# An adaLN block with linear attention and a bilinear GLU: modulation columns by halves and the first k product block by block

## The chip, the cores and the metric

The kernel runs on one core of one Trainium2 chip. The metric is the device time of one execution in microseconds; the median of three runs before the change is 566.74 us (566.28 to 568.02). Everything is computed in float32. Large products are made from float32 values that are split into a rounded high half (type fp32r, which TensorE multiplies in one pass) and a low half (value minus high half); a product of two split operands is three matmuls: high x high, high x low, low x high.

## The reference

Sequence S = 2048, width D = 512, 32 heads of 16, hidden width 1376. Cut to what matters for the change:

```python
mod = (_silu(c) @ w_mod).reshape(c.shape[0], 6, 1, -1)
sa, ca, ga, sb, cb, gb = (mod[:, 0], mod[:, 1], mod[:, 2], mod[:, 3], mod[:, 4], mod[:, 5])
h = _layernorm(x, axis=-1) * (1 + ca) + sa
x = x + ga * _A_ref(h, A_wqkv, A_wo)
h = _layernorm(x, axis=-1) * (1 + cb) + sb
x = x + gb * _B_ref(h, B_w_gate, B_w_up, B_w_down)
```

`_A_ref` is linear attention: q, k and v are products of h with the three parts of wqkv; phi(t) = where(t > 0, t + 1, exp(t)) + 1e-6 is applied to q and k; kv = sum over tokens of phi(k) times v, z = sum over tokens of phi(k); the output is (phi(q) kv) / (phi(q) z), times wo. `_B_ref` is ((h w_gate) * (h w_up)) w_down.

## The kernel before

Tokens are handled in 4 chunks of 4 token tiles of 128 tokens; D is cut into KD = 4 blocks of 128. The whole order of work is written out by hand: each engine runs its instructions in the order in which the program issues them, and waits at semaphores. Matmul results lie in two pools of four PSUM banks (`acc_bank()`, `bank()`); all large tiles in SBUF come from one pool of 99.

The opening, the part that the change touches (L342 to L474):

- All loads of the opening are issued by SyncE (SP) in one queue, in this order: chunk 0 of x (4 tiles, with c behind the first), the scale columns' part of w_mod (`raw_ca`, 4 loads of 128 x 512), the shift columns' part (`raw_sa`, 4), the k weights (`raw_k`, 4), chunk 1 of x, the q weights, the v weights, chunks 2 and 3 of x. Each is 256 KB in rows of 2 KB.
- `keep_on(n)` (L139) issues n matmuls of zeros on TensorE whose result nobody reads.
- Layer norm of chunk 0 (`Norm`): `stats` on VectorE, `rstd_of` (a power on GpSimd), `nmr_of` (minus mean times rstd, VectorE), `xhat` (the normalised tile, ScalarE), `transpose_token` (TensorE, token tile j into all four blocks' banks).
- The modulation columns: w_mod has its input rows as partition p and index k, so silu(c) @ w_mod is, per column, a sum over k and over partitions. `mod_acc` (L154) does the sum over k on VectorE, with one scale and three multiply-adds of 512 columns; `mod_col` (L161) does the sum over partitions on TensorE, four one-column matmuls against `ones`; `col_out` (L167) copies it out and adds 1 for the scale. This is done for the scale (ca), then for the shift (sa), before the first block can be modulated.
- `modulated` (L264) applies scale and shift to the transposed block k on ScalarE, and makes high and low halves; `split_raw` makes those of the weights (high on ScalarE, low on VectorE).
- The k product of token tiles 0 and 1 is `product2` (L198), two banks in turn, block by block; tiles 2 and 3 follow with `proj` (L285), one tile at a time (L424, L429).
- Then the loop over the 16 token tiles i (L425): k products two tiles ahead (`ahead`), `k_split_x` and `k_split` (high and low halves of the normalised tile and of phi(k)), `t_tile` (L325: phi(k) transposed times the normalised tile, into four accumulators `tacc`), `k_phi` and `q_a`/`q_b` (phi from a bank: two ScalarE passes and one VectorE pass), `z_add`, the next chunk's norm in pieces, and `extra[i]` (q, v and o weights' halves, the other four modulation vectors). Four q products of chunk 0 stand at i = 3, 4, 6 and 7 (`q_at`, L423).

Behind the loop come the attention output (L545 to L660), the second layer norm and the GLU (L663 to L1062), which the change does not touch.

Of the kernel before, what the change touches and what calls it, by code (L numbers as in the profile page):

```python
# [14 lines left out]
P = 128  # L15
# [7 lines left out]
def tile_adaln_block(  # L23
# [17 lines left out]
    NJ = 4  # L41
# [23 lines left out]
    def f32(ap):  # L65
        return ap.bitcast(F32)
# [33 lines left out]
    nc.gpsimd.memset(eps_z, S * EPS_PHI)  # L100
    half = consts.tile([P, NJ], F32, name="half")
# [21 lines left out]
    raw_ca = load_mod(1)  # L123
    raw_sa = load_mod(0)
    raw_k = load_qkv(1)
# [88 lines left out]
    class Norm:  # L214
# [30 lines left out]
        def xhat(self, *js):  # L245
            for j in js:
                self.n[j] = B("n")
                nc.scalar.activation(self.n[j], self.tiles[j], AF.Identity,  # L248
                                     scale=self.rstd[:, j:j + 1], bias=self.nmr[:, j:j + 1])
# [49 lines left out]

    def k_split_x(i):  # L300
# [44 lines left out]
    acc_ca, acc_sa = B("f"), B("f")  # L345
    keep_on(18)
    n0.stats(0, 1)
    n0.rstd_of(0, 2)
    silu()
    n0.stats(2)  # L350
    n0.nmr_of(0, 2)
    n0.xhat(0, 1)
    n0.stats(3)
    n0.rstd_of(2, 4)
    mod_acc(acc_ca, raw_ca, [0])
    n0.nmr_of(2, 4)
    n0.xhat(2, 3)
    n0.transpose_token(0)
    keep_on(3)
    n0.transpose_token(1)  # L360
    keep_on(3)
    n0.transpose_token(2)
    mod_acc(acc_ca, raw_ca, [1, 2, 3])
    keep_on(1)
    n0.transpose_token(3)
    ps_ca = mod_col(acc_ca, acc_bank())
    mod_acc(acc_sa, raw_sa, [0, 1, 2, 3])
    ca = col_out(1, ps_ca, 1.0)
    keep_on(4)
    ps_sa = mod_col(acc_sa, acc_bank())  # L370
    keep_on(8)
    wk.append(split_raw(raw_k[0]))
    sa = col_out(0, ps_sa, 0.0)
    nx = Norm(xts[1])
    nx.stats(0)
    n0.modulated(ca, sa, 0, cast=nc.vector)
    wk.append(split_raw(raw_k[1]))
    n0.modulated(ca, sa, 1, cast=nc.vector)
    wk.append(split_raw(raw_k[2]))
    n0.modulated(ca, sa, 2)  # L380
    nx.stats(1)
    wk.append(split_raw(raw_k[3]))
    n0.modulated(ca, sa, 3)
    ps0, ps1 = acc_bank(), acc_bank()
    product2((ps0, ps1), [[(cut(n0.t[k], j * P, (j + 1) * P), wk[k]) for k in range(KD)] for j in range(2)])
    nx.stats(2, 3)
    nx.rstd_of()
    k_split_x(0)
    k_phi(0, ps0)
    nx.nmr_of()  # L390
    k_phi(1, ps1)
    k_split(0)
    nx.xhat(0, 1)

    tacc = [acc_bank() for _ in range(KD)]
    rows, cols = {}, {}
# [7 lines left out]
    def mod_part(v, *ks):  # L404
        if 0 in ks:
# [3 lines left out]
    extra = {0: lambda: (wq.extend(split_raw(r) for r in raw_q[0:1]),),  # L409
             1: lambda: (wq.extend(split_raw(r) for r in raw_q[1:2]),),  # L410
             2: lambda: (wq.extend(split_raw(r) for r in raw_q[2:4]),),
             4: lambda: (wv.extend(split_raw(r) for r in raw_v[0:1]),),
# [10 lines left out]
    q_at = {3: 0, 4: 1, 6: 2, 7: 3}  # L423
    ahead = {2: proj(2, wk)}  # L424
    for i in range(NT):  # L425
        ch, j = divmod(i, NJ)
        more = ch + 1 < NCH
        if i == 0:
            ahead[3] = proj(3, wk)  # L429
        elif i > 1:  # L430
# [3 lines left out]
        if more and j == 0:  # L434
            nx.xhat(2)
        if i + 1 < NT:
            k_split_x(i + 1)
        if more and j == 0:
            nx.xhat(3)
# [7 lines left out]
        if ch + 2 < NCH and j == 2:  # L447
            nx2 = Norm(xts[ch + 2])
            nx2.stats(0, 1)
        if ch + 2 < NCH and j == 3:  # L450
            nx = nx2
            nx.stats(2, 3)
            nx.rstd_of()
            nx.nmr_of()
            nx.xhat(0, 1)
        if i + 2 < NT:
            k_phi(i + 2, ahead.pop(i + 2))
        else:
            q_a(i + 6 - NT, ahead.pop(i + 2))
            q_b(i + 6 - NT)  # L460
        if i in q_at:
            q_a(q_at[i], qps)
            q_b(q_at[i])
        if i + 1 < NT:
            z_add(i + 1)
        if i == NT - 1:
# [623 lines left out]
```

## Time and profile before

| | |
|---|---|
| median of three runs | 566.74 us (566.28 to 568.02) |
| the profiled execution's own time | 566.38 us |
| its span in the profile | 564.6 us |
| TensorE busy (matmul) | 556.7 us, 99% of the span |
| TensorE weight loads | 456.0 us, 81% |
| VectorE, ScalarE, GpSimd busy | 67%, 52%, 37% |
| mean granted TensorE clock | 0.995 |

The profile is of one execution. Times are microseconds from the span's start; engines are PE (TensorE matmul), PEld (its weight loads, which run beside the matmuls), DVE (VectorE), ACT (ScalarE), POOL (GpSimd) and SP (SyncE, which issues the DMAs). A line such as `L784 PE MATMUL bank<-h,w` reads: source line 784, engine, operation, written tile <- read tiles, without buffer numbers. In a timeline the columns are start, length, and then the instruction, with the idle time ahead of it and what ended it in brackets; instructions of one line that follow each other are merged (x8). Matmul lengths overlap: what one costs in a stream is the distance from one start to the next. A float32 matmul against `ones` shows as two records. The chain of waits is followed back from the end of the execution, and its rows stand in order of time. In a windows view each row is a stretch of time, with the busy time and instruction count of each engine, the granted clock (1.00 is full), the DMA engines' busy share and what they moved in GB/s.

### The profile page before, as it was taken

How to read it: one execution, taken by the hardware profiler on the slowest of the kernel's cores; microseconds unless marked ns; L12 is line 12 of the kernel's file. 1: busy time of each engine (PE TensorE's matmuls, PEld its weight loads, DVE VectorE, ACT ScalarE, POOL GpSimd, SP SyncE). 2: the span in 40 equal slices, each digit the busy share in tenths (PEclk: the TensorE clock that was granted, in tenths of full speed). 3: DMA queues.
4: the chain of work that ended last, by engine and by line, in shares of the span. 5: the costliest groups of instructions: out<-in, count | busy, mean ns of one | idle time of the engine just before them, and what ended most of it. 6: DMA issues, size and time to landing. Idle time of an engine off the chain costs nothing.

```text
span 564.6 us, 7390 instructions
## 1 busy us (share of the span) xinstructions
PE 556.7 (99%) x2549; PEld 456.0 (81%) x2549; DVE 380.2 (67%) x643; ACT 293.8 (52%) x530; POOL 207.0 (37%) x224
## 2 busy tenths in 40 slices
PE   7999999999999999999999999999999999999997
PEld 6778888887888888888888888877888888888775
DVE  6876868869898998866555767862555554444653
ACT  3685857546367877662554455453443343344420
POOL 2000000002517745345555544486324555554200
PEclk9899999999999999999999999999999999999999
DMA  8900224200421011142445134699343211200004
GB/s 270 384 17 2 74 75 140 85 0 22 128 71 43 1 48 27 38 131 94 149 150 186 39 121 169 212 350 308 113 130 102 58 48 39 80 0 1 0 1 149
DMA packets 49109, 57.24 MB, mean 101 GB/s; under 512 B 6384, under 2 KB 26864, under 8 KB 49072
## 3 DMA queue, kind: packets, MB, share of 16 engines
q1 hardware_dynamic: 49072, 56.77, 31.2%
q8 instruction: 20, 0.33, 0.2%
q14 instruction: 17, 0.14, 0.1%
HBM read 43.12 MB, written 13.63 MB: 101 GB/s over the span
## 4 chain that ended last, share of the span: by engine, by line
PE 92%; DMA 3%; DVE 3%; SPq 0%; issue 0%; ACT 0%; POOL 0%
PE bank L784 36%; PE acc L621 8%; PE acc L862 7%; PE acc L863 7%; PE acc L864 7%; PE bank L194 5%; PE bank L196 5%; PE bank L195 5%; PE acc L332 2%; PE acc L330 2%; PE acc L331 2%; PE bank L255 2%; DMA h<-side_a 1%; PE bank L596 1%; DMA x<-in_A_x_dram 1%; DMA h<-side_s 1%
## 5 line engine op out<-in xcount | busy, mean ns | idle before, releaser
L784 PE MATMUL bank<-h,w 128*128 128x512 f32 (+1 forms) x924 | 216.3, 391 | 0.2 <-DMA h<-side_s 0.2
L784 PEld LDWEIGHTS bank<-h,w 128*128 128x128 f32 (+1 forms) x924 | 170.6, 185 | 39.5 <-DMA h<-side_s 1.0
L790 ACT ACTIVATE bank<-bank 128x512 f32<-128x512 f32 (+1 forms) x44 | 25.6, 581 | 151.9 <-PE bank L784 151.8
L770 POOL TENSOR_TENSOR w<-raw,w 128x256 fp32r<-128x256 f32 (+3 forms) x44 | 46.3, 1051 | 158.4 <-ACT w L763 151.1
L810 DVE TENSOR_TENSOR phi<-bank,g 128x512 f32<-128x512 f32 (+1 forms) x22 | 15.2, 689 | 83.6 <-PE bank L784 79.9
L862 PE MATMUL acc<-w,kh 128*128 128x512 f32 (+1 forms) x176 | 68.6, 390 | 0.0
L863 PE MATMUL acc<-w,kh 128*128 128x512 f32 (+1 forms) x176 | 68.6, 390 | 0.0
L864 PE MATMUL acc<-w,kl 128*128 128x512 f32 (+1 forms) x176 | 68.5, 389 | 0.0
L770 POOL TENSOR_TENSOR w<-t,w 128x512 fp32r<-128x512 f32 (+1 forms) x44 | 57.6, 1308 | 0.0
L869 DVE TENSOR_TENSOR x<-acc,x 128x512 f32<-128x512 f32 x80 | 50.3, 682 | 8.6 <-PE acc L864 8.6
L194 PE MATMUL bank<-w,h 128*128 128x512 f32 x120 | 48.1, 401 | 0.0
L196 PE MATMUL bank<-w,h 128*128 128x512 f32 x120 | 47.0, 392 | 0.0
L195 PE MATMUL bank<-w,h 128*128 128x512 f32 x120 | 46.8, 390 | 0.0
L237 POOL TENSOR_TENSOR rstd<-ve,half 128x4 f32<-128x4 f32 (+3 forms) x12 | 11.1, 925 | 85.9 <-DVE ve L234 68.9
L490 POOL TENSOR_TENSOR f<-h,zb 128x512 f32<-128x512 f32 x12 | 17.1, 1441 | 69.4 <-ACT zb L470 50.8
L621 PE MATMUL acc<-w,xh 128*128 128x512 f32 x128 | 40.7, 399 | 0.0
L862 PEld LDWEIGHTS acc<-w,kh 128*128 128x128 f32 (+1 forms) x176 | 33.0, 188 | 7.0
L864 PEld LDWEIGHTS acc<-w,kl 128*128 128x128 f32 (+1 forms) x176 | 33.0, 188 | 7.0
L863 PEld LDWEIGHTS acc<-w,kh 128*128 128x128 f32 (+1 forms) x176 | 33.1, 188 | 6.9
L752 POOL TENSOR_TENSOR t<-raw,t 128x256 f32<-128x256 f32 (+1 forms) x44 | 36.9, 838 | 1.7
L836 DVE TENSOR_TENSOR g<-bank,u 128x512 f32<-128x512 f32 (+1 forms) x22 | 15.2, 691 | 26.7 <-ACT u L790 25.5
L248 ACT ACTIVATE n<-x,nmr,rstd 128x512 f32<-128x512 f32 x32 | 24.5, 807 | 15.3 <-DVE nmr L242 15.1
(150 smaller groups left out, 1011.9 us busy)
## 6 DMA issues: line engine op xcount, KB each, us to landing
x<-in_A_x_dram SPq DMA_DIRECT2D x24, 256.0 KB, 5.3
raw<-in_w_mod_dram SPq DMA_DIRECT2D x24, 256.0 KB, 3.6
raw<-in_B_w_gate_dram SPq DMA_DIRECT2D x40, 128.0 KB, 2.9
raw<-in_B_w_up_dram SPq DMA_DIRECT2D x40, 128.0 KB, 3.0
raw<-in_B_w_down_dram SPq DMA_DIRECT2D x20, 256.0 KB, 2.9
side_s<-h SPq DMA_DIRECT2D x16, 256.0 KB, 2.8
h<-side_s SPq DMA_DIRECT2D x16, 256.0 KB, 5.4
out_dram<-x SPq DMA_DIRECT2D x16, 256.0 KB, 2.6
```

The costliest lines, as they stand in the source:

```text
L194: nc.tensor.matmul(ps, ah, bh, start=i == 0, stop=False)
L195: nc.tensor.matmul(ps, ah, bl, start=False, stop=False)
L196: nc.tensor.matmul(ps, al, bh, start=False, stop=i == n - 1)
L621: nc.tensor.matmul(yps[i], x, y, start=fresh and k + n == 0, stop=k == KD - 1 and n == 2, skip_group_check=True)
L752: sub = lambda out, x, y: (on or nc.gpsimd).tensor_tensor(out, x, y, op=ALU.subtract)
L770: sub = lambda out, x, y: (on or nc.gpsimd).tensor_tensor(out, x, f32(y), op=ALU.subtract)
L784: mm = lambda x, y, **kw: nc.tensor.matmul(ps, x[:, k], y, skip_group_check=True, **kw)
L790: nc.scalar.activation(out, x, AF.Copy)
L862: nc.tensor.matmul(dn[j], hh[:n, a:b], dh[:n], start=i == 0, stop=False)
L863: nc.tensor.matmul(dn[j], hh[:n, a:b], dl[:n], start=False, stop=False)
L864: nc.tensor.matmul(dn[j], hl[:n, a:b], dh[:n], start=False, stop=i == n_of - 1)
L869: nc.vector.tensor_tensor(xt, dn[j], xt, op=ALU.add)
```

## The change

The shift and scale columns are made block by block. The part of w_mod for a modulation vector is loaded in halves of 256 columns (two loads of 128 x 2 x 256, rows of 1 KB), scale and shift half 0 first, then k weight 0, then halves 1, then the other k weights. Block 0 and 1 of the scale's first half are summed wholly on TensorE (`block_pe`: four accumulating one-column matmuls with the raw weights as stationary operand and silu(c) as moving column); the shift's halves and the scale's second half are summed over k on VectorE in 256-column operations (`half_dve`) and over partitions by one matmul per block (`block_one`). `block_out` copies a block's scale and shift out together and adds 1 and 0 (`unit`).

The k product of chunk 0 runs over all four token tiles at once (banks `kps`), block by block, as soon as a block is modulated (`cells`): the high half straight from the transposed block (`mod_h`), a second pass for the unrounded value (`mod_f`), the low half from both (`mod_l`). Normalised tile 3 is made on VectorE instead of ScalarE. 17 of the 37 zero matmuls are left out. The first three q products follow (with all q weights split ahead of them), each beside a `t_tile`; the fourth stands at i = 4. Token tiles 0 to 3 and the k products 4 and 5 are taken out of the loop, which begins at i = 4, and the statistics, power and normalisation of the next chunk stand one to two steps earlier in it.

The number of products of 512 columns that are not zero matmuls, of transposes and of late column sums is the same as before.

```diff
+    def load_half(v, half):
+        a = v * D + half * D // 2
+        return [load(wm_v[:, k:k + 2, a:a + D // 2], "raw") for k in range(0, KD, 2)]
...
-    raw_ca = load_mod(1)
-    raw_sa = load_mod(0)
-    raw_k = load_qkv(1)
+    raw_half[1, 0] = load_half(1, 0)
+    raw_half[0, 0] = load_half(0, 0)
+    load_k = lambda k: load(wqkv_v[k, :, D:2 * D], "raw")
+    raw_k = [load_k(0)]
+    raw_half[1, 1] = load_half(1, 1)
+    raw_half[0, 1] = load_half(0, 1)
+    raw_k += [load_k(k) for k in range(1, KD)]
...
+    def block_pe(v, b):
+        at, ps = at_of(v, b), sums_in(b)
+        for k, raw in enumerate(half_of(v, b)):
+            nc.tensor.matmul(ps[:, at:at + 1], raw, sc[:, k:k + 1], start=k == 0, stop=k == KD - 1)
+    def half_dve(v, half, *ks):
+        if 0 in ks:
+            sums[v, half] = B("f")[:, :D // 2]
+        mod_acc(sums[v, half], [raw_half[v, half][k // 2][:, k % 2] for k in range(KD)], ks)
+    def block_one(v, b):
+        at = at_of(v, b)
+        nc.tensor.matmul(sums_in(b)[:, at:at + 1], sums[v, b // 2][:, b % 2 * P:(b % 2 + 1) * P], ones[:, 0:1],
+                         start=True, stop=True)
+    def block_out(b):
+        nc.vector.tensor_tensor(both[:, b], sums_in(b)[:, 2 * b:2 * b + 2], unit, op=ALU.add)
+    def mod_h(k):
+        halves[k] = (B("h", dt=F32R), B("h", dt=F32R), B("f"))
+        h, l, f = halves[k]
+        nc.scalar.activation(h, n0.ps[k], AF.Identity, scale=ca[:, k:k + 1], bias=sa[:, k:k + 1])
...
+    def mod_l(k):
+        h, l, f = halves.pop(k)
+        nc.vector.tensor_tensor(l, f, f32(h), op=ALU.subtract)
+        n0.t[k] = (h, l)
...
+    def cells(*tk, parts=(0, 1, 2)):
+        for part in parts:
+            for t, k in tk:
+                h, l = halves[k][:2] if k in halves else n0.t[k]
+                x, w = ((h, wk[k][0]), (h, wk[k][1]), (l, wk[k][0]))[part]
+                nc.tensor.matmul(kps[t], x[:, t * P:(t + 1) * P], w, start=k == 0 and part == 0,
+                                 stop=k == KD - 1 and part == 2)
     keep_on(18)
...
+    n0.xhat(0, 1)
+    k_split_xh(0)
     n0.stats(3)
     n0.rstd_of(2, 4)
+    n0.transpose_token(0)
     n0.nmr_of(2, 4)
+    n0.xhat(2)
+    n0.xhat(3, on=nc.vector)
+    keep_on(2)
     n0.transpose_token(1)
+    block_pe(1, 0)
+    half_dve(0, 0, 0, 1, 2, 3)
+    weight_h(0)
     n0.transpose_token(2)
     n0.transpose_token(3)
+    block_one(0, 0)
+    block_out(0)
+    weight_l(0)
+    mod_h(0)
+    mod_f(0)
+    block_pe(1, 1)
+    block_one(0, 1)
+    half_dve(1, 1, 0, 1)
+    block_out(1)
+    half_dve(1, 1, 2, 3)
+    mod_l(0)
...
+    cells((0, 0), (1, 0), parts=(0, 1))
+    cells((2, 0), (3, 0), parts=(0, 1))
+    cells(*four(0), parts=(2,))
+    mod_h(1)
+    mod_f(1)
+    weight_h(1)
+    half_dve(0, 1, 0, 1, 2, 3)
+    weight_l(1)
+    mod_l(1)
+    k_split_xh(1)
+    cells(*four(1), parts=(0,))
+    block_one(1, 2)
+    block_one(0, 2)
+    block_one(1, 3)
+    block_one(0, 3)
+    cells(*four(1), parts=(1, 2))
+    weight_h(2)
+    block_out(2)
+    block_out(3)
+    weight_l(2)
+    mod_h(2)
+    mod_f(2)
+    weight_h(3)
+    mod_l(2)
+    mod_h(3)
+    weight_l(3)
+    mod_f(3)
+    k_split_xl(0)
+    mod_l(3)
+    cells((0, 2), (1, 2))
...
+    cells((3, 3))
+    k_split_xl(1)
...
+    wq_go(0, 1, 2)
+    k_phi(0, kps[0])
+    wq_go(3)
+    k_split(0)
+    nx.stats(0)
+    k_phi(1, kps[1])
+    nx.stats(1)
+    k_phi(2, kps[2])
+    k_split(1)
     nx.stats(2, 3)
     nx.rstd_of()
     nx.nmr_of()
...
+    qps = proj(0, wq)
+    t_tile(0, *range(KD))
+    k_phi(3, ps3)
+    nx.xhat(0, 1)
+    q_a(0, qps)
+    q_b(0)
+    nx.xhat(2, 3)
+    qps = proj(1, wq)
+    k_split_x(2)
+    k_split(2)
+    t_tile(1, *range(KD))
+    qps2 = proj(2, wq)
+    z_add(1)
+    k_split_x(3)
+    nx.transpose(0, 1)
+    nx.modulated(ca, sa, 0, 1, cast=nc.vector)
+    q_a(1, qps)
+    q_b(1)
+    t_tile(2, *range(KD))
+    k_split(3)
+    nx.transpose(2, 3)
+    nx.modulated(ca, sa, 2, 3, cast=nc.vector)
...
+    t_tile(3, *range(KD))
+    ahead[4] = proj(4, wk)
...
+    for i in range(4, NT):
```

More of the change, by code (lines that the diff above doesn't have):

```diff
@@ L100, in tile_adaln_block @@
     nc.gpsimd.memset(eps_z, S * EPS_PHI)
+    unit = consts.tile([P, 2], F32, name="unit")
+    nc.gpsimd.memset(unit[:, 0:1], 1.0)
+    nc.gpsimd.memset(unit[:, 1:2], 0.0)
     half = consts.tile([P, NJ], F32, name="half")
@@ L346, in tile_adaln_block @@
     keep_on(18)
-    n0.stats(0, 1)
+    n0.stats(0)
+    silu()
+    n0.stats(1)
     n0.rstd_of(0, 2)
-    silu()
     n0.stats(2)
@@ new lines, in tile_adaln_block @@
+    mod_h(0)
[6 more added lines that the diff above has]
+    mod_l(0)
+    kps.update({t: acc_bank() for t in range(2)})
+    kps[2] = ps_idle
+    kps[3] = bank()
+    four = lambda k: [(t, k) for t in range(NJ)]
+    cells((0, 0), (1, 0), parts=(0, 1))
[6 more added lines that the diff above has]
+    weight_l(1)
@@ L381, in tile_adaln_block, with wq_go @@
+    cells((3, 3))
+    k_split_xl(1)
+    nx = Norm(xts[1])
+    def wq_go(*ks, low=None):
+        wq.extend(split_raw(raw_q[k], low=low) for k in ks)
+    wq_go(0, 1, 2)
+    k_phi(0, kps[0])
+    wq_go(3)
+    k_split(0)
+    nx.stats(0)
+    k_phi(1, kps[1])
     nx.stats(1)
[L382 to L385, printed above, removed]
+    k_phi(2, kps[2])
@@ L465, in tile_adaln_block @@
             z_add(i + 1)
+        if ch + 2 < NCH and j == 2:
+            nx2.nmr_of()
+            nx2.xhat(0, 1)
+        if ch + 2 < NCH and j == 3:
+            nx.xhat(3)
         if i == NT - 1:
```

123 lines of the change are left out of this document (77 added, 46 removed).

## The prediction

> **What bounds the kernel now.** I read the page's shares first, then the chain of waits over the opening, then TensorE's and the other engines' timelines, then the same stretch in windows.
>
> ```profile
> span 564.6 us, 7390 instructions
> ...
> PE 556.7 (99%) x2549; PEld 456.0 (81%) x2549; DVE 380.2 (67%) x643; ACT 293.8 (52%) x530; POOL 207.0 (37%) x224
> ...
> PE 92%; DMA 3%; DVE 3%; SPq 0%; issue 0%; ACT 0%; POOL 0%
> ```
>
> TensorE sets the end, but its 99% counts filler (L141 multiplies zeros). So the question is when the first useful product starts and whether TensorE ever waits after it. Chain of waits, opening:
>
> ```profile
> 2.66 5.87 DMA x<-in_A_x_dram
> ...
> 9.74 0.88 POOL rstd L237
> ...
> 10.74 0.76 DVE f L159
> ...
> 15.88 1.16 PE acc L164 x8
> 17.04 3.43 PE acc L141 x8
> 20.46 0.47 PE acc L204 x2
> ```
>
> The last x tile lands at 8.53, the layer norm follows until 10.6, VectorE builds both modulation sums until 15.8, and the first product (L204) starts only at 20.30. TensorE's timeline:
>
> ```profile
> 16.90 3.57 PE L141 MATMUL acc<-w 128*128 128x512 f32 x8
> 20.30 0.63 PE L204 MATMUL acc<-w,h 128*128 128x512 f32 x2
> ...
> 25.78 0.39 PE L194 MATMUL bank<-w,h 128*128 128x512 f32 x1
> ...
> 31.22 0.39 PE L330 MATMUL acc<-kh,xh 128*128 128x512 f32 x1
> ...
> 38.46 0.40 PE L194 MATMUL bank<-w,h 128*128 128x512 f32 x1
> ...
> 41.78 0.40 PE L330 MATMUL acc<-kh,xh 128*128 128x512 f32 x1
> ```
>
> The 48 matmuls of the first four k products run from 20.30 to 31.22 without a wait: 10.92/48 = 0.2275 us each. The 12 of 38.46 to 41.78 take 3.32 where 12 x 0.2275 = 2.73, so 0.6 us is lost there. Windows along the clock's own steps:
>
> ```profile
> 3.25:6.66 3.41, 3.41 (x9) 2.62 (x9) 1.57 (x3) 0.21 (x1) 0.00 (x0) 1.00 0.90 256
> 6.66:10.07 3.41, 2.53 (x14) 1.85 (x13) 3.03 (x12) 1.52 (x2) 1.04 (x2) 1.00 0.94 314
> 10.07:13.49 3.42, 3.29 (x22) 2.41 (x20) 2.75 (x5) 1.53 (x2) 0.54 (x1) 1.00 1.05 406
> 13.49:16.90 3.41, 2.81 (x20) 2.28 (x19) 2.92 (x5) 0.63 (x1) 0.00 (x0) 0.97 1.05 384
> 16.90:20.31 3.41, 3.41 (x10) 2.69 (x11) 3.05 (x8) 3.04 (x5) 0.00 (x0) 0.53 1.04 384
> 160.00:564.60 404.60, 400.39 (x1820) 328.28 (x1818) 254.80 (x417) 198.65 (x375) 189.01 (x197) 1.00 0.31 100
> ```
>
> Columns: stretch, length, busy us and count of PE, PEld, DVE, ACT, POOL, clock, DMA share, GB/s. After 13.49:16.90, in which TensorE ran mostly one-column sums (L164) and four fillers, the granted clock is 0.53 for one step and full again behind it. From 160 us on TensorE is busy 400.4 of 404.6, and neither the diff nor the instruction order touches that part: what the opening gains or loses arrives at the end.
>
> **Part 1: an earlier first product.** The prices:
>
> ```profile
> 9.57 0.48 DVE L157 TENSOR_SCALAR f<-raw,sc 128x512 f32<-128x512 f32 x1
> 10.64 0.16 DVE L242 SCALAR_TENSOR_TENSOR nmr<-mv,rstd 128x2 f32<-128x2 f32 x1 [0.59 <-POOL rstd L237]
> 10.74 2.33 DVE L159 SCALAR_TENSOR_TENSOR f<-raw,sc,f 128x512 f32<-128x512 f32 x3
> ...
> 17.07 0.16 DVE L169 TENSOR_SCALAR col<-acc 128x4 f32<-128x4 f32 x1 [0.58 <-PE acc L164]
> ...
> 18.57 0.69 DVE L274 TENSOR_TENSOR h<-f,h 128x512 fp32r<-128x512 f32 x1
> 19.18 0.69 DVE L182 TENSOR_TENSOR w<-raw,w 128x512 fp32r<-128x512 f32 x1
> ```
> ```profile
> 14.66 0.63 ACT L181 ACTIVATE w<-raw 128x512 fp32r<-128x512 f32 x1 [2.30 <-DMA raw<-in_A_wqkv_dram]
> 17.27 0.78 ACT L269 ACTIVATE f<-bank,col,col 128x512 f32<-128x512 f32 x1 [1.97 <-DVE col L169]
> ```
>
> The x loads keep their place in SP's queue, so the second nmr stays at 10.64 and ends at 10.80. Then on VectorE: the normalised tile 3, moved there from ScalarE, 0.48 (to 11.35); the shift sum of the first half, one scale and three multiply-adds of 256 columns. No row has 256 columns. Half of the 512-column rows gives 0.24 + 3 x 0.376 = 1.4, the full rows 2.7; on a straight line between the 2-column rows (0.16) and the 512-column ones (0.48 and 0.75) it is 0.32 + 3 x 0.45, with issue gaps 1.8, which I take: 13.15. Then one ones-sum on TensorE (0.39 by 1.16 us for four with 0.255 apart) 13.6, block_out 0.16 to 13.85, the rounded modulated block on ScalarE 0.78: **first product at 14.7** (14.3 to 15.6), against 20.30: **-5.6**. A hand-over between engines costs 0.03 to 0.06 in these rows (17.04 to 17.07, 17.23 to 17.27).
>
> Hidden beside this: block_pe, four one-column matmuls at 0.22 to 0.255, waits for the first scale half, but the transposes behind it wait for tile 2 from ScalarE anyway (n at 10.85 + 0.8 = 11.65); if that half were late by 1 us, the transposes and all behind would be too. The first k weight had eight 256 KB loads ahead of it and landed at 14.66; now it has four, at the rows' pace:
>
> ```profile
> 423.00:425.00 2.00, 2.00 (x11) 1.65 (x10) 0.00 (x0) 1.03 (x2) 2.00 (x3) 1.00 1.03 278
> 12.00:14.00 2.00, 1.87 (x17) 1.52 (x15) 1.93 (x4) 0.37 (x1) 0.00 (x0) 1.00 1.06 405
> ```
>
> At 12 to 14 us the queue moves 2 KB rows at 405 GB/s, 0.65 us for 256 KB. The half loads have 1 KB rows, which no row shows; at 423 us the queue moves mostly 512 B rows of the gate and up weights at 278 GB/s, 0.94 us. So a half load costs 0 to 0.29 us more; I take 0.1. The weight lands at 14.66 - 4 x 0.65 + 4 x 0.1 = 12.4 (13.2 at the dear end), its copy 0.63 later, before the modulated block at 13.85. Hidden. The new memsets of `unit` on GpSimd are done before 3 us, far ahead of use.
>
> **Part 2: four tiles block by block.** The 48 matmuls still cost 10.92. Added among them: four ones-sums, 4 x 0.235 = 0.9. VectorE must have the low halves ready: from 13.8 it does four subtractions at 0.6, eight 256-column operations (2 x 1.8) and a small one, so block 1's low half comes at about 20.0 while TensorE, 12 + 8 matmuls and the sums on, asks for it at 21.4. Block 2 and 3 need both column pairs (20.8), then on ScalarE two 0.67-spaced passes each and one weight copy; the last low half is ready at 24.9, TensorE wants it at 24.7: 0.2 of waiting. Now the clock: 18 + 2 fillers remain where there were 37, and 10.2 to 14.7 holds 12 transposes, ten one-column sums and no filler, thinner than 13.49:16.90 was. I expect a half-clock step from 13.49 to 16.90, as behind that window. It meets 2.2 us of product: +1.1 (bounds 0 and, with a second step, +2.8). Sum: 10.9 + 0.9 + 0.2 + 1.1 = 13.1, the block ends at 27.9 against 31.22: **-3.3**.
>
> On the clock the Trainium skill speaks against this change: "TensorE: Matmul & The Clock Gate", Part 4, says that the full clock does not engage for transposes, and its table "Why this matters for your kernels" asks for some 4 us of unbroken matmuls before the full clock. By it a product begun at 14.7 would meet the full clock only at the step of 20.31, the rival "two half steps" below. The trace neither proves nor refutes it: 10.07:13.49 held 12 transposes and kept the clock, but with seven fillers among them.
>
> **Part 3: q products behind it.** The same products in another order; the 0.6 us at 38.46 goes. What is late next is token tile 3. Spacing rows (L274 to L182, 0.60) price VectorE: from 24.3 two low halves, four q weights, three phi, two kl at 0.6 = 6.6, four statistics (0.73 + 0.10 each) 3.3, small waits 0.6: 34.8. Then the power on GpSimd, nmr 36.1.
>
> ```profile
> 26.04 1.38 POOL L237 TENSOR_TENSOR rstd<-ve,half 128x4 f32<-128x4 f32 x1 [15.43 <-DVE ve L234]
> 51.59 1.01 POOL L237 TENSOR_TENSOR rstd<-ve,half 128x4 f32<-128x4 f32 x1 [24.16 <-DVE ve L234]
> ...
> 52.83 1.52 ACT L248 ACTIVATE n<-x,nmr,rstd 128x512 f32<-128x512 f32 x2 [5.48 <-DVE nmr L242]
> ```
>
> Behind nmr ScalarE has four normalisations (0.72 apart), two phi pairs, two tile splits, two kh and two modulated blocks, about 9.3 to 45.5, then VectorE 1.3: kl of tile 3 at 46.8. TensorE, 72 matmuls and 16 transposes (0.11 apart) after 27.9, is there at 46.5. Wait 0.3, or 0.6 if the power takes 1.38. Normalising chunk 2 and 3 works the same way with some 0.1 and 0.3 of waiting. Added 0.6 (0 to 2.0), removed 0.6: **0**. Two fewer late q products in the loop only move.
>
> **Sum.** -3.3 against the profiled execution's 566.38 (1.8 around its span): 563.1. That execution is 0.36 below the median of 566.74, so I put the prediction at **563.4**.
>
> **Rivals.**
> *Two half steps* (18%): the clock returns only at 20.31, because the window 13.49:16.90 is only 64% product. For it: the window from 3.25 that brought the clock back in the start was wholly busy. Against: 6.66:10.07 kept it at 2.53 of 3.41. Half of a further 3.41 is 1.7: 565.1. The Trainium skill's rule above gives this one.
> *No half step* (14%): the transposes and sums hold the clock, +1.1 falls away: 562.3.
> *The new chain becomes the bound, slower* (12%): token tile 3's chain of some 15 VectorE and 14 ScalarE instructions has no slack left (46.8 against 46.5). It decides as soon as instructions run at their full length (0.69, 0.63, 0.80) instead of the spacing (0.60, 0.53, 0.72): some 0.09 x 29 = 2.6 here, and about half of that again at each later hand-over to chunks 2 and 3: 563.4 + 5.2 = 568.6. For it: the queue is in order and every instruction moves TensorE. Against: the spacing held in a stage where VectorE had no air:
>
> ```profile
> 38.46:49.96 11.50, 11.50 (x50) 8.85 (x48) 11.36 (x22) 6.79 (x12) 0.00 (x0) 1.00 0.01 2
> ```
>
> *It doesn't bring the product forward* (8%): 1 KB rows at half pace, 0.65 more each. The fourth half load then lands 2.6 later, the weight at 14.7 and scale and shift of blocks 2 and 3 some 5 us later; TensorE stalls in mid-product and ends it near 30.8: about 566.
>
> **How the numbers follow.** Forecast 48%, own range 562.4 to 564.4. Under 0.3%, 1.7 us, this kernel cannot be told from no change, so faster means below 565.04, slower above 568.44. Faster: 48 + 14 and a quarter of the 18%: 0.66. Same: the rest of the 18% and the 8%: 0.22. Slower: 0.12. The range 561.8 to 566.4 takes in both clock cases, the dear 256-column and 1 KB ends and most of the last rival, and leaves out the slow chain.
>
> **What would show it.** Right: first product at 14.3 to 15.6, its last matmul near 28, clock near 0.5 in one step around 14 to 17, waits at tile 3 below 1 us. Wrong: the scale and shift columns of blocks 2 and 3 later than 21.5, VectorE without a gap from 24 to 47 and TensorE waiting there for over 2 us, or half clock after 17.

## The result, and the profile after

The changed kernel's median is 562.77 us (560.88 to 565.19, nine runs) against 565.95 us (565.29 to 568.02, nine runs) for the kernel before: ratio 0.9942, 95% interval 0.9925 to 0.9960. That is 3.2 us less by the medians; 563.4 and -3.3 were forecast. The profiled execution of the changed kernel took 561.47 us, 4.9 less than the profiled one of before. It is one of the quicker of the nine: of the 1.7 between its 4.9 and the median's 3.2, 1.3 lie on the side of the changed kernel (562.77 against 561.47), mostly by the clock, as the runs below show, and 0.4 on the side of before.

The page of the profile after, its totals and the shares of the chain of waits:

```profile
span 559.8 us, 7391 instructions
PE 551.9 (99%) x2544; PEld 453.5 (81%) x2544; DVE 379.8 (68%) x648; ACT 294.2 (53%) x531; POOL 207.4 (37%) x226
PE 94%; DVE 3%; DMA 1%; SPq 0%; issue 0%; ACT 0%; POOL 0%
```

TensorE still sets the end; the loads' share of the whole chain fell from 3% to 1%. TensorE's timeline after, from the first column sums to the first q product (L439 is `cells`, L399 a ones-sum, L388 the scale's columns on TensorE, L206 the q product):

```profile
13.58 0.35 PE L399 MATMUL acc<-ones,f 128*128 128x1 f32 x2 [0.56 <-DVE f L171]
13.80 1.03 PE L388 MATMUL acc<-sc,raw 128*128 128x1 f32 x8
...
15.00 1.43 PE L439 MATMUL acc<-w,h 128*128 128x512 f32 x5
...
16.72 0.39 PE L439 MATMUL bank<-w,h 128*128 128x512 f32 x1
17.22 0.96 PE L439 MATMUL acc<-w,h 128*128 128x512 f32 x3
...
19.17 0.95 PE L399 MATMUL acc<-ones,f 128*128 128x1 f32 x8
19.98 0.96 PE L439 MATMUL acc<-w,h 128*128 128x512 f32 x3
...
27.52 0.39 PE L206 MATMUL bank<-w,h 128*128 128x512 f32 x1
```

The first product stands at 15.00 (before: 20.30) and the first q product at 27.52 (before: 31.22). In between lie 12.52 us: 48 matmuls at 0.2275 are 10.92, the four ones-sums 19.98 - 19.17 = 0.81, and the rest is 0.79, nearly all of it in five short waits, of which the longest is at 16.72: its successor comes 0.50 later instead of 0.23, because block 0's low half is late.

What stood ahead of the first product, on VectorE:

```profile
10.87 0.16 DVE L254 SCALAR_TENSOR_TENSOR nmr<-mv,rstd 128x2 f32<-128x2 f32 x1 [0.81 <-POOL rstd L249]
11.07 0.55 DVE L261 TENSOR_SCALAR n<-x,rstd,nmr 128x512 f32<-128x512 f32 x1
11.53 0.34 DVE L169 TENSOR_SCALAR f<-raw,sc 128x256 f32<-128x256 f32 x1
11.91 1.52 DVE L171 SCALAR_TENSOR_TENSOR f<-raw,sc,f 128x256 f32<-128x256 f32 x3
13.97 0.16 DVE L403 TENSOR_TENSOR both<-acc,unit 128x2 f32<-128x2 f32 x1 [0.54 <-PE acc L399]
```

and on ScalarE:

```profile
12.64 0.63 ACT L427 ACTIVATE w<-raw 128x512 fp32r<-128x512 f32 x1 [0.76 <-DMA raw<-in_A_wqkv_dram]
14.17 0.78 ACT L410 ACTIVATE h<-bank,both 128x512 fp32r<-128x512 f32 x1 [0.90 <-DVE both L403]
```

The chain is the forecast one, link for link: nmr, tile 3, shift sum, ones-sum, `both`, the modulated block. The weight's copy (12.64) is done long before the block (14.17). Windows after, along the same steps as before's (columns as there):

```profile
10.07:13.49 3.42, 2.51 (x21) 2.15 (x19) 2.42 (x6) 1.70 (x3) 0.70 (x1) 1.00 1.09 364
13.49:16.90 3.41, 3.32 (x20) 2.84 (x20) 2.85 (x8) 2.71 (x4) 0.00 (x0) 1.00 1.06 382
...
160.00:559.80 399.80, 395.69 (x1798) 324.95 (x1796) 251.53 (x411) 196.16 (x370) 189.10 (x196) 1.00 0.32 101
```

The clock is full in every row: this execution has no half-clock step in the opening. (The profile of before has one, on its last fillers and ahead of its first product.) Counted back from its last matmul, TensorE stands 4.2 us ahead of before from about 85 us on (the 1600th matmul from the end starts at 198.53 against 202.72), and 4.9 us ahead from about 420 us on. The last 0.7 is no part of the change's work: in before TensorE waited once at 382 us for a load (0.18 idle, and the matmuls on both sides further apart than 0.23), and not in the profile after. TensorE's timeline there, before:

```profile
379.64 2.65 PE L784 MATMUL bank<-h,w 128*128 128x512 f32 x10
382.46 1.87 PE L784 MATMUL bank<-h,w 128*128 128x512 f32 x7 [0.18 <-DMA h<-side_s]
```

Two of the profiles below (with eight fillers, and with none) show the same wait in changed kernels, so it comes and goes between executions.

### The profile page after: what moved, and what is told of

The parts are those of the page before. It is cut to its first block, busy times and chain, and to the rows that moved or that the text cites. A ratio compares the mean times of both kernels' runs of the same rounds, so it can differ in the third digit from the quotient of the medians.

```text
span 559.8 us, 7391 instructions
## 1 busy us (share of the span) xinstructions
PE 551.9 (99%) x2544; PEld 453.5 (81%) x2544; DVE 379.8 (68%) x648; ACT 294.2 (53%) x531; POOL 207.4 (37%) x226
## 4 chain that ended last, share of the span: by engine, by line
PE 94%; DVE 3%; DMA 1%; SPq 0%; issue 0%; ACT 0%; POOL 0%
PE bank L970 38%; PE acc L807 8%; PE acc L1048 7%; PE acc L1049 7%; PE acc L1050 7%; PE bank L206 5%; PE bank L207 5%; PE bank L208 5%; PE acc L357 2%; PE acc L355 2%; PE acc L356 2%; PE bank L271 2%; PE acc L439 1%; DMA x<-in_A_x_dram 1%; PE bank L782 1%; PE acc L271 1%
## 5 line engine op out<-in xcount | busy, mean ns | idle before, releaser
L206 PE MATMUL bank<-w,h 128*128 128x512 f32 x112 | 44.8, 400 | 0.0
L208 PE MATMUL bank<-w,h 128*128 128x512 f32 x112 | 43.7, 390 | 0.0
L207 PE MATMUL bank<-w,h 128*128 128x512 f32 x112 | 43.6, 390 | 0.0
L249 POOL TENSOR_TENSOR rstd<-ve,half 128x4 f32<-128x4 f32 (+3 forms) x12 | 11.2, 930 | 83.0 <-DVE ve L246 71.4
```

Source lines behind the costliest of these rows:

```text
L206: nc.tensor.matmul(ps, ah, bh, start=i == 0, stop=False)
L207: nc.tensor.matmul(ps, ah, bl, start=False, stop=False)
L208: nc.tensor.matmul(ps, al, bh, start=False, stop=i == n - 1)
```

## The experiments

Twelve runs. The first four ask what the clock does, since the forecast put one half-clock step into its sum and the profile after has none.

### The changed kernel as it is, again

No edit.

> The changed kernel once more, beside the next three. Clock theory: its executions so far spread from 560.9 to 565.2 us, and the mean granted clock falls from 1.000 to 0.994 along with it; a step of 3.41 us at half clock is 0.003 of the mean and costs half of it at most, 1.7 us. So I expect again some 561 to 565 us, median near 562.8, with every execution at a clock of 1.000 within 0.5 us of 561.2 and those at 0.994 near 564.5. Rival: the spread has nothing to do with the clock (loads, say); then time and clock do not go together.

Measured: 562.69 us (560.38 to 564.77, 12 runs), ratio 0.9934 (0.9906 to 0.9962). The profiled execution took 564.76 us, 3.3 more than the earlier profile of the same program. Its windows, along the steps of this execution's own clock, and TensorE's timeline:

```profile
10.60:14.01 3.41, 2.05 (x16) 1.65 (x15) 2.45 (x7) 1.45 (x2) 0.70 (x1) 1.00 1.08 361
14.01:17.42 3.41, 3.23 (x14) 3.17 (x15) 2.05 (x7) 1.76 (x3) 0.00 (x0) 0.50 1.03 365
17.42:20.83 3.41, 3.41 (x10) 2.64 (x9) 3.27 (x8) 2.70 (x5) 0.00 (x0) 0.50 0.90 248
```
```profile
14.61 1.84 PE L388 MATMUL acc<-sc,raw 128*128 128x1 f32 x8
...
16.74 2.48 PE L439 MATMUL acc<-w,h 128*128 128x512 f32 x5
```

Two half-clock steps in a row: the one-column sums ahead of the product take 1.84 instead of 1.03, the first product comes at 16.74 instead of 15.00, and its matmuls lie 0.43 apart until 20.8. The clock's steps do not begin at the same place of the program in each execution: its half-clock step runs from 16.68 to 20.09 in the profile of before, and the two here from 14.01 to 20.83. The other windows of this section and of the result lie 0.2 us behind the steps of before, so that a clock such as 0.98 or 0.52 in a row belongs to a window that cuts a step. Of the 3.3 us, 0.61 are not clock: the second nmr starts at 11.48 here and at 10.87 there. Sorted by their mean granted clock, the 21 runs of the changed kernel so far fall into three groups. One half-clock step of 3.41 us takes 0.5 x 3.41 / 560 = 0.003 off the mean; the clock can also be halved for the last 2 us or so, behind the last matmul, where it costs nothing and takes up to 0.002 off (the profile of before ends with 1.8 us at 0.50):

```
mean clock        runs   median us
0.998 to 1.000      6      561.10
0.995 to 0.997      8      562.64
0.992 to 0.994      7      564.03
```

None, one and two steps occur about equally often; the medians of the second and third group lie 1.5 and 2.9 us above that of the first, later landings of the x tiles included.

### Four fillers more

```diff
     block_pe(1, 0)
+    keep_on(1)
     half_dve(0, 0, 0, 1, 2, 3)
...
     n0.transpose_token(3)
+    keep_on(3)
     block_one(0, 0)
```

> Four zero matmuls put back into TensorE's two idle stretches, 11.5 to 11.9 and 12.8 to 13.6 us. They take 0.9 us of a gap of 1.0, so they may delay the first product by 0 to 0.2 us. Clock theory: the thin stretch from 10.2 to 15.0 loses its half steps in part of the executions: median 561.3 to 562.0, spread smaller than without. Rival (the clock is ruled by the long mean, or the spread is from elsewhere): median as without, 562.8, or 0.2 later.

Measured: 561.84 us (561.12 to 562.68, 7 runs), ratio 0.9922 (0.9893 to 0.9951); and in a second comparison:

> The changed kernel with the four fillers once more, on the same chip as the two others. If four fillers keep the clock, the mean clock is 0.998 or more in nearly all runs and the median 561.6 to 562.2 at a ratio near 0.992; if the first time was luck, clocks of 0.992 to 0.997 come up in half of the runs, as without them, and the median is 562.7.

Measured: 561.33 us (560.41 to 565.59, 6 runs), ratio 0.9913 (0.9879 to 0.9946). Of the 13 runs 12 have a mean clock of 0.998 or more, against 6 of 21 without the four fillers. The thin window in the first profile with them:

```profile
10.07:13.49 3.42, 3.38 (x26) 2.75 (x24) 2.64 (x8) 1.45 (x2) 0.00 (x0) 1.00 1.09 364
```

The fillers close the idle time between 10 and 13.5 us (busy 3.38 of 3.42, against 2.51 without) and TensorE is not needed for anything else then. The half-clock steps go in nearly all runs. The gain of about 1 us by the medians (561.8 against 562.8) lies inside the two intervals against before, so it is the clocks, 12 of 13 against 6 of 21, that carry the finding.

### Eight fillers more, and none

```diff
+    keep_on(3)
     block_pe(1, 0)
...
     n0.transpose_token(3)
+    keep_on(5)
```
```diff
-    keep_on(2)
     n0.transpose_token(1)
```

> Eight zero matmuls there, 1.8 us at full clock, of which some 0.9 us does not fit into the idle time and delays the first product. Clock theory: every execution near clock 1.000 behind the start, time 561.9 to 562.4 with a spread under 1 us. Rival: 563.7, the old median and the 0.9 us, with the old spread.

> The last two zero matmuls (behind the first tile's transposes) taken out too. The queue gives the same times without the clock, since they stand in idle time. Clock theory: more executions with one or two half steps, median 563.5 to 564.5, mean clock 0.994 to 0.997. Rival: as changed, 562.8.

Measured with eight: 562.14 us (561.77 to 562.64, 8 runs), ratio 0.9928 (0.9901 to 0.9955), all clocks 0.998 or more. With none: 562.66 us (561.31 to 564.37, 12 runs), ratio 0.9941 (0.9920 to 0.9963); one run without a step, six with one, five with two. Eight are no better than four: in that profile the ones-sum stands behind the fillers, and the first product comes 4.5 us behind nmr instead of 4.1 without the four and 4.3 in their first profile (their second has 4.5 too, behind an early nmr). Taking the change's own two fillers out was to be worse and is not: they run near 9.6 us, ahead of the thin stretch, and what they do there was not settled.

### Three adds ahead of the next chunk's statistics

From here on the four fillers stay in, so that the clock does not blur the differences. The adds' result is not used.

```diff
     k_split(0)
+    late = B("f")
+    for _ in range(3):
+        nc.vector.tensor_tensor(late, xts[1][0], xts[1][0], op=ALU.add)
     nx.stats(0)
```

> Changed kernel with the four fillers (561.84 us alone), and three needless 128x512 adds on VectorE ahead of the first statistics of the next four token tiles. Three adds at the 0.60 us spacing are 1.8 us, and VectorE has no gap from 22 to 34 us, so the adds arrive in full at the statistics. My theory: the chain to token tile 3 (statistics, power, normalisation, phi, kl) has no slack against TensorE, which reaches it within 0.1 us of its being ready: TensorE then waits 1.8 us or a little more near 45 us, time 563.6 to 564.0. Rival: there is slack there, or the later stages take the delay back: 561.6 to 562.2.

Measured: 564.45 us (563.19 to 569.16, 10 runs), ratio 0.9954 (0.9914 to 0.9994); over the seven runs at 0.998 or more the median is 564.30, against 561.77 for the twelve with the fillers alone: +2.5. TensorE's waits in the stretch from 13 to 60 us:

```profile
PE acc L355 <- DVE phi L314: 1.0, 2, 0.6
```

and its timeline:

```profile
30.72 0.39 PE L357 MATMUL acc<-kl,xh 128*128 128x512 f32 x1
31.69 0.50 PE L355 MATMUL acc<-kh,xh 128*128 128x512 f32 x1 [0.58 <-DVE phi L314]
...
46.78 0.40 PE L356 MATMUL acc<-kh,xl 128*128 128x512 f32 x1
47.29 0.50 PE L357 MATMUL acc<-kl,xh 128*128 128x512 f32 x1
```

Nothing is taken back in this stretch: the adds take 2.1 us on VectorE (0.69 apart and not 0.60), and TensorE stands 1.8 us behind the profile with the fillers alone from 47 to 123 us. At the end it is 1.2, since the profile with the fillers alone loses 0.8 near 135 us that this one does not (see the run on GpSimd's multiplications). The profiled execution is also the quickest of the seven; what makes the others' 2.5 is not explained. But the wait is not where I had put it. Most of it falls at 31 to 33 us, where TensorE wants the phi that stand behind the adds and the statistics on VectorE (0.97 and 0.82 between matmuls that are 0.23 apart in the stream), and only 0.3 is left for token tile 3 at 46.8. VectorE's whole queue from 22 to 34 us is next to without slack, not only the chain to tile 3.

### The scale's first half on VectorE

```diff
-    block_pe(1, 0)
+    half_dve(1, 0, 0, 1, 2, 3)
...
+    block_one(1, 0)
     block_one(0, 0)
...
-    block_pe(1, 1)
+    block_one(1, 1)
     block_one(0, 1)
```

> Changed kernel with the four fillers, but the first half of the scale columns is summed on VectorE as the shift's is (one scale, three multiply-adds of 256 columns, 1.9 us by the rows of the changed kernel) and no longer by 16 one-column matmuls on TensorE. My theory: VectorE is what the first product waits for, so the first product comes 1.8 us later (16.2 us for 14.4) and the end too: 563.6; with a half-clock step on top up to 565.3. Rival: what brought the first product forward is the layer norm and the halves, and the place of the scale sum is hidden: 561.6 to 562.2.

Measured: 566.34 us (563.64 to 568.39, 10 runs), ratio 0.9980 (0.9943 to 1.0018). The three runs at 0.998 or more have 563.76, +2.0 against the fillers alone; the others carry one to three half-clock steps. TensorE's timeline:

```profile
13.33 0.35 PE L399 MATMUL acc<-ones,f 128*128 128x1 f32 x2
15.06 0.83 PE L399 MATMUL acc<-ones,f 128*128 128x1 f32 x6 [1.38 <-DVE f L171]
16.50 0.74 PE L439 MATMUL acc<-w,h 128*128 128x512 f32 x2 [0.62 <-ACT h L410]
```

TensorE waits 1.38 for the second half sum, and the first product comes at 16.50 for 14.39. Of these 2.1 us, 0.55 are the second nmr, which starts at 10.62 here and at 10.07 in the profile with the fillers; behind nmr the product comes 1.6 later. So the scale's first sum on TensorE is worth 1.6 us in the profiles and 2.0 by the runs at full clock, of which there are only three; the median lies another 2.6 above that, by half-clock steps.

### Tile 3 normalised on ScalarE

```diff
-    n0.xhat(2)
-    n0.xhat(3, on=nc.vector)
+    n0.xhat(2, 3)
```

> Changed kernel with the four fillers, and the last of the first four token tiles is normalised on ScalarE again, behind the third. VectorE gets 0.55 us back ahead of the shift sum; ScalarE's tile 3 ends 0.8 us later and its transposes with it. My theory: VectorE's shift sum sets the first product, which comes 0.4 us sooner (14.0 for 14.4), and if that lasts the time is 561.4; but TensorE already waits 0.34 us for VectorE's low halves near 135 us in the run with four fillers, so half of it or all may be lost there: 561.4 to 561.8. Rival: the later transposes set the modulated block, first product not sooner or later by up to 0.3: 561.8 to 562.2.

Measured: 561.92 us (561.57 to 567.00, 10 runs), ratio 0.9911 (0.9868 to 0.9955): the same as with the fillers alone. VectorE's timeline says why:

```profile
11.10 1.52 DVE L171 SCALAR_TENSOR_TENSOR f<-raw,sc,f 128x256 f32<-128x256 f32 x3
13.74 0.16 DVE L403 TENSOR_TENSOR both<-acc,unit 128x2 f32<-128x2 f32 x1 [1.12 <-PE acc L399]
```

The shift sum ends 2.16 us behind the start of nmr (2.56 in the changed kernel), but now `both` waits 1.12 instead of 0.54 for the ones-sum, which stands in TensorE's queue behind the last four transposes (late by ScalarE) and three fillers. With these fillers in the queue the place of tile 3 is worth nothing by itself.

### Two token tiles first

The order of the kernel before: all four blocks for tiles 0 and 1, then for 2 and 3.

```diff
-    cells((2, 0), (3, 0), parts=(0, 1))
-    cells(*four(0), parts=(2,))
+    cells(*two(0), parts=(2,))
...
-    cells((0, 2), (1, 2))
...
-    cells((3, 3))
+    cells(*two(2))
+    cells(*two(3))
+    for t in (2, 3):
+        for k in range(KD):
+            cells((t, k))
```

> Changed kernel with the four fillers, but the first k product takes all four blocks for token tiles 0 and 1 first and then tiles 2 and 3, as the kernel before did. Blocks 2 and 3 are then wanted after 24 matmuls and not 48. Their columns come near 20.2 us, and ScalarE and VectorE need two passes, a weight copy and two low halves for each. My theory (walked through with the trace's durations): TensorE waits about 2.7 us for blocks 2 and 3, the last k matmul ends near 29.7 us for 27.0, time 564.5. Rival: the matmuls are the same ones, the wait goes elsewhere or the q products take it up: 561.6 to 562.4.

Measured: 568.22 us (565.23 to 570.49, 10 runs), ratio 0.9993 (0.9950 to 1.0036), that is no gain over before left. The single run at full clock has 565.23, +3.5; nine of ten have half-clock steps. TensorE's waits, 13 to 160 us:

```profile
PE acc L439 <- DVE h L422: 1.0, 1, 1.0
PE acc L399 <- DVE f L171: 0.5, 1, 0.5
```

and a window: 

```profile
20.31:23.70 3.39, 3.39 (x9) 2.62 (x9) 2.54 (x7) 3.35 (x6) 0.00 (x0) 0.50 1.05 386
```

The wait comes a step sooner than I had it: with two tiles there are four matmuls and not eight in front of block 0's low half, so TensorE waits 1.0 for that one, and 0.5 for the second half's sums; then the half clock (from 19.2 to 26.0 in this execution) slows TensorE so much that blocks 2 and 3 are there in time. The size held only for the one run without half clock, of which there is no profile. What is shown is that four tiles cover block 0's low half and the second half's sums; that they cover the columns of blocks 2 and 3 fits the total of that run and is not shown.

### The kernel before with fewer fillers

The change also drops fillers. Dropped alone, from the kernel before:

```diff
-    keep_on(4)
...
-    keep_on(8)
```

> The kernel before, without its two later filler groups (4 and 8 matmuls of zeros ahead of the modulated blocks, which the change also drops); nothing else. TensorE waits for VectorE's sums and for ScalarE there either way. My theory: the gain is the earlier columns, not the dropped fillers; without them the first product of before starts 0.5 to 1 us sooner at most (19.3 to 19.8 us for 20.3), and less cover invites half-clock steps: 564.7 to 567.5, ratio 0.998 to 1.003. Rival: the fillers held the first product back, so dropping them alone brings most of the gain: 562.5 to 563.5, ratio 0.994 to 0.996.

Measured: 567.59 us (566.24 to 573.98, 12 runs), ratio 1.0022 (0.9994 to 1.0050); all 12 clocks below 0.995. Windows:

```profile
13.49:16.90 3.41, 1.40 (x12) 1.23 (x11) 2.70 (x6) 0.76 (x2) 0.00 (x0) 0.98 1.05 381
16.90:20.31 3.41, 1.92 (x5) 1.54 (x6) 3.10 (x7) 3.41 (x6) 0.00 (x0) 0.50 1.05 385
20.31:23.70 3.39, 3.39 (x10) 2.66 (x9) 3.35 (x7) 2.66 (x5) 0.00 (x0) 0.52 1.06 387
```

The first product comes at 18.39 for 20.30, more than I had allowed, but TensorE is busy only 1.40 of 3.41 ahead of it and the clock is halved for two steps. So some 1.8 of the 5.3 us by which the change brings the first product forward are fillers: in the profile of before eight of them run at half clock until 20.30, and the block's high half is ready at 18.53. Left out of the kernel before, they still bring no time. At an equal clock (0.992 to 0.994) ten of these runs have a median of 567.5 us, and before has 568.6 in its two such runs of this comparison and 567.8 in the twelve of all four: on these few runs the fillers hold back 0.3 to 1 us, and the lost clock takes it back. Dropping them alone is not where the gain comes from.

### GpSimd's multiplications out of VectorE's way

In the first profile with four fillers the lead of 0.5 us over the changed kernel's profile turned into a lag of 0.25 near 135 us. VectorE's, GpSimd's and TensorE's timelines in that profile:

```profile
128.52 1.82 DVE L678 TENSOR_TENSOR f<-h,zb 128x512 f32<-128x512 f32 x1
...
130.98 0.68 DVE L678 TENSOR_TENSOR f<-h,zb 128x512 f32<-128x512 f32 x1
```
```profile
127.26 2.53 POOL L678 TENSOR_TENSOR f<-h,zb 128x512 f32<-128x512 f32 x2 [49.23 <-ACT zb L658]
```
```profile
135.69 0.33 PE L207 MATMUL bank<-w,w 128*128 128x128 f32 x1 [0.34 <-DVE w L194]
```

One VectorE multiplication takes 1.82 for 0.68 while GpSimd does the same work on other tiles, and TensorE then waits for VectorE's low halves. The edit moves two of GpSimd's multiplications behind a third that becomes ready at 137 us:

```diff
     den_z()
-    den_p(1, 0, 1)
     den_a(0, 0, 1, on=nc.vector)
...
     den_p(1, 2)
+    den_p(1, 0, 1)
```

> Changed kernel with the four fillers, and two of GpSimd's multiplications for the denominators (tiles 4 and 5) moved behind a third one, so that they no longer run while VectorE multiplies at 128 to 131 us. In the profile with four fillers VectorE's multiplication that met them took 1.82 us and the one behind it 0.68; VectorE was late with the low halves near 135 us and TensorE lost 0.7 us of its lead there. My theory: the two engines hold each other up; apart, VectorE is there 0.4 to 1.1 us sooner, the lead of the earlier opening comes through to the end: 561.1 to 561.5, against 561.8 with the fillers alone. Rival: the multiplications collide with VectorE's next work instead, or VectorE is as late for another reason: 561.7 to 562.5.

Measured: 561.24 us (560.88 to 562.10, 5 runs), ratio 0.9905 (0.9877 to 0.9933). VectorE after the edit:

```profile
128.52 0.69 DVE L678 TENSOR_TENSOR f<-h,zb 128x512 f32<-128x512 f32 x1
129.84 0.68 DVE L678 TENSOR_TENSOR f<-h,zb 128x512 f32<-128x512 f32 x1
```

Both now take 0.69 and 0.68, and there is no wait near 135 us. That wait is no fixed part of the unedited program, though: in its second profile VectorE's two multiplications take 0.68 and 1.06 and GpSimd's two 3.07 instead of 2.53, and TensorE does not wait near 135 us either. Against that profile the edited one gains 0.5 us between 130 and 139 us, against the first 1.2. Against the changed kernel's profile TensorE is 0.06 us ahead at 55 us and 0.53 ahead at 139 us, and 0.45 at the end. The time (561.24) cannot be told from the fillers alone on the same chip (561.33): the mechanism is shown, its worth of about half a microsecond only in the profiles.

### Tile 3 on ScalarE, fillers ahead of its transposes

```diff
-    n0.xhat(2)
-    n0.xhat(3, on=nc.vector)
+    n0.xhat(2, 3)
...
-    keep_on(1)
+    keep_on(2)
...
+    keep_on(1)
     n0.transpose_token(3)
-    keep_on(3)
```

> The version with the later denominators (561.24 us), but the last of the first four token tiles is normalised on ScalarE as in e6, and the fillers stand ahead of its transposes (two after the block's column sums, one between tiles 2 and 3) and none behind them. In e6 VectorE had the shift sum 0.4 us sooner but the ones-sum stood in TensorE's queue behind the last transposes and three fillers (0.8 us). My theory: with these three fillers out of the way the modulated block comes 4.0 us behind the last nmr and not 4.3, which is worth 0.3 to 0.4 us at full clock: 560.8 to 561.0; and the clock holds, as TensorE is busy there nearly as before. Rival: three fillers are too few there, half-clock steps come back in a third of the runs or more, and the median is 562.0 or above. A third outcome, no difference (561.1 to 561.5), would mean that the time goes by the landing of the last x tile, which moves by more than this from run to run.

Measured: 561.38 us (560.58 to 561.71, 6 runs), ratio 0.9921 (0.9900 to 0.9942), all clocks 0.998 or more: no difference, the third outcome. The reason named with it is only half of it: nmr came early in this profile, and VectorE then met the next bound.

```profile
9.99 0.16 DVE L254 SCALAR_TENSOR_TENSOR nmr<-mv,rstd 128x2 f32<-128x2 f32 x1 [0.81 <-POOL rstd L249]
11.22 0.36 DVE L169 TENSOR_SCALAR f<-raw,sc 128x256 f32<-128x256 f32 x1 [1.07 <-DMA raw<-in_w_mod_dram]
```

The shift's half load lands only at 11.2, and VectorE waits 1.07 for it. From here the opening hangs on the load queue. The kernel with four fillers and the three variants of it that move only tile 3's normalisation or GpSimd's multiplications (medians 561.24 to 561.92) are all quicker than the kernel before. Their medians are also below that of the changed kernel as it is, but the intervals overlap; which of them is best these runs do not tell.

## Why the prediction was right, step by step

**First product.** Forecast 14.7 (14.3 to 15.6), measured 15.00. Of the 0.3 missing, 0.23 is the last x tile: nmr starts at 10.87 and not at 10.64, as the landing of that tile moves between executions. It moves by up to 1.8 us over the profiles here, so that a hit within 0.3 is luck in part; what the forecast has right is the way from nmr to the product, 4.06 forecast and 4.13 measured. The rest is the sum's own small change: VectorE's tile 3 has 0.55 and not 0.48, and the multiply-adds of 256 columns lie 0.52 apart where 0.45 was the row's length put in, so that the shift sum takes 1.9 for 1.8. The weight's landing (forecast 12.4, copy starts at 12.64) is hidden as said, and the half loads' price holds: 364 GB/s in the window 10.07 to 13.49, in which the weight's 2 KB rows land among the 1 KB ones, against 406 before, 0.07 us more for 256 KB against the 0.1 taken. The rival of 1 KB rows at half pace falls.

**The block.** 10.92 for the 48 matmuls and 0.81 for the sums stand as forecast (10.9 and 0.9). The waits are 0.8 and not 0.2: the mis-sized term is block 0's low half, for which no wait had been reckoned, and four hand-overs of 0.11 to 0.13. (14.7 and the sum's 13.1 give 27.8, not the 27.9 that was written.) The half-clock step is right as the typical case and wrong as a certainty: 8 of 21 runs have one, 6 none and 7 two. Its price, +1.1, measures 1.5 by the medians, that of two 2.9 against the bound of 2.8; the step also slows the column sums ahead of the product, which the forecast left out. The case forecast as likeliest lies in the middle of what the same program does, so the median fell on it; that it fell so near to 563.4 is luck in part. I had given "two steps" 18% and "none" 14% as if one of them were the kernel's fate; each is a third of its executions.

On the rule from the Trainium skill that spoke against the change ("TensorE: Matmul & The Clock Gate", Part 4 and the table "Why this matters for your kernels"): that the full clock does not engage for transposes would have led to two steps. 7 of 21 runs have the clock of two steps. In the profile after, TensorE kept full clock through 12 transposes and a window busy 2.51 of 3.42, so the rule names a risk here and no certainty; an unbroken 4 us of matmuls was not needed to keep a clock that was already full.

**Behind the block.** Forecast 0 (0.6 gained near 38 us, 0.6 lost at tile 3); the profile gives -0.5. The 0.6 came, since the lead grows from 3.70 at the first q product to 4.2 near 85 us. The wait did not. VectorE's and TensorE's rows:

```profile
35.20 0.17 DVE L254 SCALAR_TENSOR_TENSOR nmr<-mv,rstd 128x4 f32<-128x4 f32 x1 [1.12 <-POOL rstd L249]
...
45.31 0.68 DVE L347 SCALAR_TENSOR_TENSOR kl<-phi,kh 128x512 fp32r<-128x512 f32 x1
```
```profile
46.08 0.46 PE L357 MATMUL acc<-kl,xh 128*128 128x512 f32 x1
46.38 0.39 PE L355 MATMUL acc<-kh,xh 128*128 128x512 f32 x1
```

kl of tile 3 is ready at 45.99 (46.8 forecast), and TensorE takes it at 46.08 and loses 0.07. Two mis-sized terms, VectorE's run to the statistics (nmr at 35.2 for 36.1) and TensorE's start (27.5 for 27.9), nearly cancel. (The forecast's 46.5 is 0.5 more than its 72 matmuls and 16 transposes give; the two matmuls of tile 3 that stand ahead of kl make the difference.) That there is next to no slack, on which the slower rival stood, the three adds show for VectorE's queue as a whole: 1.8 of their 2.1 us arrive, most of it ahead of tile 3's chain. The rival's condition, instructions at full length, did not come about.

**The sum.** Equal clocks can be compared where both kernels ran side by side, in the comparison of the changed kernel as it is: without a step 564.99 us (12 runs of before) and 561.17 (3 runs), with one 565.82 (7) and 562.50 (4), with two 567.14 (5) and 564.03 (5). So at equal clock the change is worth 3.8, 3.3 and 3.1 us. Over more comparisons (561.10 for the six runs without steps, 565.30 for 34 of the 74 runs of before in three of them) it is 4.2, but these mix chips whose medians of before differ by up to 1.2. The 4.2 of the two profiles are not at equal clock, since the one of before has a step and the one after has none; the forecast was made from that profile of before, and without its own half-clock step it is -3.3 - 1.1 = -4.4. Of the parts, the four-tile order is worth most (3.5 without it, by the one run at full clock), the scale's sum on TensorE 1.6 to 2.0, the place of tile 3 nothing. They add up to more than the whole; that each covers waits which the other would leave is my reading and was not tested. The half loads and the new order of the q products were not taken back alone; what the q products brought shows behind the block only, 0.5 of the profile's 4.2.

## What to carry to other kernels

Work brought forward into an opening also thins TensorE there: after such a change, sort the runs by their mean granted clock before explaining a spread, and put fillers only into the idle time that the window shows and no more than fit, since the awaited work stands behind them in the queue. When columns or weights arrive block by block, spread each block over more output tiles, so that the matmuls of one block cover the making of the next. A queue without gaps on a helper engine is a bound even at 68% over the span: three adds of 2.1 us in it came out 1.8 us later on TensorE.

## What the runs showed of the hardware

- The same program takes none, one or two half-clock steps of 3.41 us in different executions, in about equal parts, and the steps begin at another place of the program in each. How busy TensorE was in the step ahead does not settle it. On each execution's own steps, 2.81 of 3.41 (from 13.27) lost the clock in before and 2.05 lost it in the changed kernel's second profile, while 2.44 (from 10.14) kept it in the first, and the version with the scale on VectorE kept it through two thin steps in a row:

```profile
8.44:11.85 3.41, 1.97 (x13) 1.52 (x14) 2.37 (x8) 2.86 (x4) 0.75 (x2) 1.00 1.08 375
11.85:15.26 3.41, 2.03 (x15) 1.64 (x14) 2.98 (x7) 0.63 (x1) 0.00 (x0) 1.00 1.09 369
15.26:18.67 3.41, 2.77 (x14) 1.97 (x13) 3.12 (x9) 2.98 (x5) 0.00 (x0) 1.00 1.05 384
```

  What decides it stays open.
- VectorE's and GpSimd's multiplications of two SBUF tiles hold each other up: VectorE's takes 1.82 for 0.68 in one profile and 0.69 with GpSimd's moved away, and in another profile GpSimd's two take 3.07 for 2.53. The Trainium skill ("SBUF — State Buffer", section "SBUF: two separate sides") states that the two share a pair of ports under an exclusive lock, and that the later one waits for the other's whole instruction; the trace agrees with that, since VectorE's ends 0.55 us behind GpSimd's second one (at 130.34 and 129.79).
- The start of nmr, and with it the landing of the last x tile, moves between 9.68 and 11.48 us over these profiles of programs that load it in the same place of the queue. In the changed kernel and with fillers added or taken out, the first product follows 4.1 to 4.5 us behind it where the clock is full.
